# A scan, a routed expert layer and a Fourier mix in one kernel: the routing's PE steps, the last scatters and three small pieces of work in another order

## The chip, the cores and the metric

The kernel runs on one core of a Trainium2 chip. A core has five engines that work from queues of their own, each in the order in which the program was written: TensorE (PE, matrix products; PEld is its loading of weights), VectorE (DVE), ScalarE (ACT), GpSimd (POOL), and SyncE (SP), which here only issues DMAs. GpSimd issues the indirect DMAs (scatters by row number). An instruction waits at the head of its queue until its operands are there and its output's buffer is free, and whatever is behind it waits too. The metric is device time in microseconds (us), the median of several runs.

## The reference, cut to what matters

Three stages follow each other, each on the whole output of the one before (batch 4, 768 positions, width 256).

```
# 1. a scan with decay: 8 heads of 32, state 16; x, a, B, C are inputs, chunks of the sequence are carried by a state
y[i] = sum over j <= i in the chunk of (C_i . B_j) * exp(cum_i - cum_j) * x[j]  +  C_i . state * exp(cum_i)
state = decay_full * state + sum over j of B_j x_j * exp(cum_last - cum_j)
# 2. routing to one of 8 experts per token, with a gate that may keep the previous token's expert
fresh = argmax(x @ w_gate);  e = fresh if s == 0 or sigmoid(x @ w_local) < 0.5 else previous e
out = softmax(x @ w_gate)[e] * (relu(x @ w1[e]) @ w2[e])           # w1: 256 x 1024, w2: 1024 x 256
# 3. mixing and a feed-forward layer
u = x + real(fft(fft(x, axis=1), axis=2));  un = layernorm(u)
out = u + relu(un @ w_ch1) @ w_ch2                                 # 256 x 1024, 1024 x 256
```

## The kernel before, in words

The order of all work is written out by hand: the code is run once in the order in which it stands, and each engine's queue gets its instructions in that order.

**The scan** (0 to about 88 us) goes over 12 pairs: six chunks of 128 positions, and in each the batches 0, 1 and 2, 3. In pair i PE makes the scores of pair i+1 (L438, tiles `g`), the sums of pair i over the chunk (L469, into `yb`), which ScalarE copies to `x1t` (L476), the products for the state of pair i+1 (`state_mm`, L484, into the PSUM bank `mb`), and then two products of the rows of pair i (`tl`, L522, which read `x1t`) around the carry (L458). VectorE meanwhile makes the masks of the next pair (`mt`, L446), which the sums read.

**The routing** of a chunk that is done runs beside the following pairs. It is a generator cut into steps: "v" steps (VectorE's, called by `gap()`) and "p" steps (PE's, called by `place()`). A first "p" step transposes the keep-and-fresh numbers `kd` (L560), which ScalarE copies to `kr` (L570); VectorE scans them; a second transposes the result (L581), copied to `f_` (the chosen expert) by ScalarE at L583; VectorE makes a one-hot array of it (L593) and running counts; a third multiplies (L608, L609) to get ranks; VectorE turns ranks into row numbers `si` (L636). All "p" steps write to the same PSUM bank `mb` as the state products. Each turn of the pair loop calls `place()` three times, once near the beginning (ahead of the sums) and twice between the row products; a chunk's routing therefore goes forward by a "p" step at each. The last chunk is routed in two halves of two batches.

When `si` is there, GpSimd scatters a batch's 128 rows to `xs_buf`, a buffer in HBM ordered by expert (L643, by `leave()` or at the end). Behind the scatters of the last but one chunk, SP loads the first 256 rows of expert 0 from there into `xe` (L649); the scatters of the last chunk (four, one per batch) follow.

**The experts** run in turn: 0 on the 256 rows in `xe`, then 0 to 7 on the rest of their rows, which SP loads once the last scatter has landed. For each, the rows are transposed (L979) and split in a high and a low part (ScalarE, VectorE L982); weights come by SP and are split too, high by ScalarE (L207) and low by VectorE (L210). Products with the first weights (L918, tiles `mm`) turn in three PSUM buffers; ScalarE takes the relu `hh` (L924), VectorE the low part `hl` (L925); products with the second weights follow (L960). Expert 0's remaining 128 rows go another way: 12 products (L896), relu `hr` (L901), transposes (L908). A `hook(i)` is called behind each of 12 steps of an expert (or of a group of the mixing stage); tables say which piece of side work is issued in which hook (`PREP`, `SORT`, `plan`). Side work is among others the splitting of eight chunks of constants (`prep_steps`: VectorE L144 to L147, ScalarE L153, GpSimd L157 and L158), and the sort that prepares the two last experts (`sort_rows`, scatters to `xs_part` at L1054).

**The mixing stage**: `stage_b(b, k2)` (L1429) makes two products into a PSUM buffer `mix`, from which VectorE and ScalarE read; the last layer's results are `o` (VectorE, L1511). Products with the constants are again L918 and L960.

Of the kernel before, what the change touches and what calls it, by code (L numbers as in the profile page):

```python
# [16 lines left out]
NC = S // 128  # L17
# [7 lines left out]
EARLY = 256  # L25
# [7 lines left out]
MORE = {0: 8, 1: 10}  # L33
PREP = tuple((c, (e, 6), (e, 9)) for c, e in enumerate((1, 2, 3, 4, 5)))
PREP += ((5, (NE - 2, 7), (NE - 2, 9)), (6, (1, 9), (1, 10)), (7, (NE - 2, 9), None))
SORT = {(1, 8): 2, (1, 9): 1, (1, 10): 3, (2, 8): 2, (2, 9): 1, (2, 10): 3}

FT = (
    (((0, 0),), ((0, 1),)),
# [19 lines left out]
def tile_kernel(ctx: ExitStack, tc: tile.TileContext, io):  # L59
# [41 lines left out]
    def disjoint(name, w):  # L101
        if name in groups:
            tc.declare_no_dep(w.ins, group=name, reason="the rows of a scatter are its own")
        groups.add(name)
        tc.add_to_no_dep_group(name, w.ins)
# [13 lines left out]
    def prep_steps(i, pool):  # L119
        n = 512  # L120
        w = i // 4
        q = i % 4
        if w == 0:
            src = io["wc1"][(q // 2) * 128:(q // 2) * 128 + 128, (q % 2) * n:(q % 2 + 1) * n]
            dst = [t[:, q // 2, (q % 2) * n:(q % 2 + 1) * n] for t in wch[0:2]]
            sh = [128, n]
            raw = wraw.tile([128, n, 2], I32, tag="raw", name="rawc")
            SP.dma_start(out=raw.rearrange("p f t -> p (f t)"), in_=src.bitcast(I32))
        else:
            src = io["wc2"][q * 256:q * 256 + 256, :]  # L130
            dst = [t[:, 2 * q:2 * q + 2, :] for t in wch[2:4]]
            sh = [128, 2, D]
            raw = wraw.tile([128, n, 2], I32, tag="raw", name="rawc")
            SP.dma_start(
                out=raw.rearrange("p (k d) t -> p k (d t)", k=2),
                in_=src.bitcast(I32).rearrange("(k p) d -> p k d", p=128),
            )
            dst = [t.rearrange("p k d -> p (k d)") for t in dst]
        yield
        hw, lw = raw[:, :, 1], raw[:, :, 0]  # L140
        v = pool.tile([128, n], I32, tag="cv", name="cv")
        e = pool.tile([128, n], I32, tag="ce_", name="ce_")
        r = pool.tile([128, n], FP32, tag="cr", name="cr", bufs=1)
        V.tensor_scalar(out=e, in0=hw, scalar1=3, scalar2=0x3FFFFFF8, op0=ALU.logical_shift_left, op1=ALU.bitwise_and)  # L144
        V.scalar_tensor_tensor(out=v, in0=hw, scalar=-0x40000000, in1=e, op0=ALU.bitwise_and, op1=ALU.bitwise_or)
        V.tensor_scalar(out=e, in0=v, scalar1=-0x800000, scalar2=None, op0=ALU.bitwise_and)
        V.scalar_tensor_tensor(  # L147
            out=r, in0=lw.bitcast(mybir.dt.uint32), scalar=2.0 ** -52, in1=e.bitcast(FP32), op0=ALU.mult, op1=ALU.mult
        )
        vf = v.bitcast(FP32)  # L150
        if i == 6:
            yield
        A.activation(out=dst[0], in_=vf, func=ACTF.Copy)  # L153
        yield
        ef = e.bitcast(FP32)
        eng = G if i else V
        eng.tensor_tensor(out=ef, in0=vf, in1=dst[0], op=ALU.subtract)  # L157
        eng.tensor_tensor(out=dst[1], in0=ef, in1=r, op=ALU.add)  # L158
        yield

# [84 lines left out]
    def phase_a():  # L245
        with ExitStack() as st:
# [281 lines left out]
            def routing(c, b0, nb):  # L528
# [112 lines left out]
                def leave(bb):  # L641
                    for b in bb:
                        w = G.indirect_dma_start(  # L643
                            out=xs_buf, out_offset=bass.IndirectOffsetOnAxis(ap=si[:, b:b + 1], axis=0),
                            in_=x1n[:, b0 + b, 0:RW], in_offset=None, bounds_check=NE * NTOK - 1, oob_is_err=False,
                        )
                        disjoint("xs", w)
                    if c + 2 == NC and bb[-1] + 1 == nb:
                        SP.dma_start(out=xe, in_=xs_buf[0:EARLY, :].rearrange("(t p) r -> p t r", p=128))  # L649

                for b in range(0, nb, 2):
                    scq.append((leave, range(b, b + 2), now[0]))
# [63 lines left out]
            for i, (c, bp) in enumerate(pairs):  # L716
                now[0] += 1
                more = i + 1 < NP
                last = i + 2 >= NP
# [17 lines left out]
                if more:  # L737
                    scores(i + 1)
                if not last:
                    place()  # L740
                    prep(i + 2)
                intra(i)
                keep(i)
                if last:
                    place()
                if not more:
                    next(ws)
                if not more:
# [392 lines left out]
    def experts():  # L1141
# [4 lines left out]
            next(od)  # L1146
        xn = load_x(pools, 0)
        xn1 = load_x(pools, 1)
        keep_clock(ps2, 4)
        early = split_t((xp, pst), lambda t, d: xe[:, t, 137 * d:137 * d + 128], n=EARLY)  # L1150
        for _ in ws:
# [3 lines left out]
        def first(i):  # L1155
            nonlocal nxt, ws
            if 0 < i < 4:
                next(od)
            if i == 0:
                ws = load_w(1)  # L1160
            if i == 6:
                past(out_e, cc("rid")[:, 0:2], nfirst.to_broadcast([128, 2]))
                tokens(ids_e, xe, out_e, 2)
            if i == 8:
                nxt = split_x(pools, xn, out_of[:, 0, :], CAPS[0])
# [3 lines left out]
        for e in range(NE):  # L1169
# [7 lines left out]
            def hook(i):  # L1177
                nonlocal nxt, ws, nr
                if (e, i) in ((1, 0), (2, 4)):
                    srt[:] = [sort_rows(pools, SORTED[e - 1])]  # L1180
                    next(srt[0])
                for _ in range(SORT.get((e, i), 0)):
                    next(srt[0])
                if (e, i) == (1, 9):
                    sq = sm.tile([128, 1], FP32, tag="sq", name="sq", bufs=1)
                    A.activation(out=sq, in_=ident[:, 0:1], func=ACTF.Sqrt)
                if (e, i) == (4, 8):
                    nr = rounds(sm)
                    next(nr)
                if (e, i) == (4, 10):  # L1190
                    nr = next(nr)
                at = AT.get(e, (2, 3, 4, 5, 8, 8))
                for _ in range(at.count(i) if more else 0):
                    next(ws, None)
                for c, x, y in PREP:
                    if (e, i) == x:
                        chunk[c] = prep_steps(c, sm)
                        next(chunk[c])
                    if (e, i) == y:
                        next(chunk[c])  # L1200
                        if c != 6:
                            next(chunk[c])
                if (e, i) == (1, 11):
                    next(chunk[6])
                    next(chunk[6])
                if more and (e, i) == (e, MORE.get(e, 9)):
                    next(ws, None)
                    ws = load_w(e + 2) if e + 2 < NE else None
                if i == 7 and more:
                    nxt = split_x(pools, xn, out_of[:, e + 1, :], CAP if e + 1 == last - 1 else CAPS[e + 1])  # L1210
# [57 lines left out]
    def transform(lead):  # L1268
# [303 lines left out]
        def turn(i):  # L1572
# [39 lines left out]
        plan = {  # L1612
# [3 lines left out]
        }  # L1616
        for g, b in ((2, 2), (3, 3)):
            for k, v in (
# [136 lines left out]
```

## Time and profile before

| | |
|---|---|
| median of 3 runs | 424.89 us (423.1 to 426.29) |
| the profiled execution | 426.76 us, span 425.0 us, mean granted clock 0.996 |
| PE busy | 402.1 us, 95% of the span |
| PEld | 353.8 us, 83% |
| DVE | 281.8 us, 66% |
| ACT | 188.3 us, 44% |
| POOL | 147.7 us, 35% |
| chain that ended last | PE 74%, DVE 12%, ACT 6%, DMA 5%, issue 2% |

The span is the time from the first to the last record of the profiled execution; its device time is 1.8 us longer. Busy times are those in which an engine worked on an instruction; they overlap between engines. The chain is followed back from the last instruction to what released each step, so its shares tell what the end depended on, not what was busy. Rows of a timeline tell, in brackets, how long an engine had been idle before an instruction and what released it.

### The profile page before, as it was taken

To read this page: it belongs to the slowest core of one execution; us is meant where nothing else is said; L and a number is where in the kernel's file an instruction comes from. 1 tells how busy PE (TensorE), PEld (TensorE's weight loads), DVE (VectorE), ACT (ScalarE), POOL (GpSimd) and SP (SyncE) were. 2 spreads that over 40 slices of the span, in tenths; PEclk is the share of its full clock that TensorE was granted. 3 is DMA by queue.
4 is the path that set the end of the run, shared out by engine and by line. 5 is a ranking of instruction groups with operands and counts; after the bars stand their busy time and mean duration, and the time that the engine had idled before them with its cause. 6 is when DMAs were issued, how large, how long until landed. Compare 5 with 4: busy or idle time off the path is not lost.

```text
span 425.0 us, 8313 instructions
## 1 busy us (share of the span) xinstructions
PE 402.1 (95%) x3113; PEld 353.8 (83%) x3113; DVE 281.8 (66%) x770; ACT 188.3 (44%) x409; POOL 147.7 (35%) x206
## 2 busy tenths in 40 slices
PE   8898898788799999999999999999999999999995
PEld 4576566568689989999998998798898998989885
DVE  4678878873577897676865668875576685743431
ACT  3355465523656546474675425423324344331220
POOL 1264876641001717533253606325402713200000
PEclk9999999999899999999999999999999999999999
DMA  8798454224782957586663410452113010000101
GB/s 278 245 325 279 133 173 140 78 77 148 235 280 93 261 182 238 165 260 219 168 225 99 135 56 28 139 184 56 56 39 87 15 39 0 28 25 14 37 15 42
DMA packets 34089, 56.26 MB, mean 132 GB/s; under 512 B 3318, under 2 KB 23063, under 8 KB 34040
## 3 DMA queue, kind: packets, MB, share of 16 engines
q1 hardware_dynamic: 30328, 46.82, 34.7%
q0 software_dynamic: 3200, 8.54, 5.7%
q8 instruction: 26, 0.43, 0.4%
q10 hardware_dynamic: 512, 0.28, 0.2%
q14 instruction: 23, 0.19, 0.1%
HBM read 42.60 MB, written 13.17 MB: 131 GB/s over the span
## 4 chain that ended last, share of the span: by engine, by line
PE 74%; DVE 12%; ACT 6%; DMA 5%; issue 2%; POOL 0%; SPq 0%; ACTq 0%; DVEq 0%
PE mm L918 25%; PE mm L960 20%; PE mm L936 9%; PE tl L522 3%; DMA r<-in_w_dram 3%; PE tp L979 2%; PE f L1371 2%; DVE mt L446 2%; PE g L438 2%; PE mb L286 2%; PE yb L469 1%; DVE w1l L210 1%; DVE hl L925 1%; ACT w1h L207 1%; ACT x1t L476 1%
## 5 line engine op out<-in xcount | busy, mean ns | idle before, releaser
L925 DVE SCALAR_TENSOR_TENSOR hl<-mm,hh 128x512 fp32r<-128x512 f32 (+7 forms) x112 | 65.9, 593 | 48.2 <-ACT hh L924 47.9
L924 ACT ACTIVATE hh<-mm 128x512 fp32r<-128x512 f32 (+7 forms) x112 | 57.5, 521 | 72.6 <-PE mm L918 72.6
L960 PE MATMUL mm<-c2h,hh 128*128 128x256 f32 x192 | 54.4, 283 | 0.0
L960 PE MATMUL mm<-c2h,hl 128*128 128x256 f32 x192 | 53.8, 280 | 0.1
L960 PE MATMUL mm<-c2l,hh 128*128 128x256 f32 x192 | 53.6, 279 | 0.0
L918 PE MATMUL mm<-xh,w1h 128*128 128x288 f32 (+6 forms) x128 | 41.9, 335 | 1.8 <-DVE hl L925 1.4
L1075 POOL DMA_INDIRECT y_tok<-y,ids x26 | 26.9, 1034 | 45.3 <-ACT y L1074 23.3
L918 PE MATMUL mm<-xh,w1l 128*128 128x288 f32 (+6 forms) x128 | 40.5, 323 | 0.0
L918 PE MATMUL mm<-xh,c1h 128*128 128x512 f32 x96 | 38.8, 404 | 0.1
L918 PE MATMUL mm<-xh,c1l 128*128 128x512 f32 x96 | 38.0, 396 | 0.0
L960 PEld LDWEIGHTS mm<-c2h,hl 128*128 128x128 f32 x192 | 36.1, 188 | 0.3 <-DVE hl L925 0.3
L960 PEld LDWEIGHTS mm<-c2l,hh 128*128 128x128 f32 x192 | 36.1, 188 | 0.1
L960 PEld LDWEIGHTS mm<-c2h,hh 128*128 128x128 f32 x192 | 36.1, 188 | 0.1
L446 DVE TENSOR_TENSOR mt<-g,ca 128x512 f32<-128x512 f32 x48 | 31.4, 677 | 4.8 <-PE g L438 4.7
L918 PE MATMUL mm<-xl,w1h 128*128 128x288 f32 (+6 forms) x128 | 31.2, 324 | 0.0
L210 DVE TENSOR_TENSOR w1l<-r,w1h 128x512 fp32r<-128x512 f32 x32 | 24.3, 763 | 10.0 <-ACT w1h L207 9.8
L918 PE MATMUL mm<-xl,c1h 128*128 128x512 f32 x96 | 30.1, 395 | 0.0
L643 POOL DMA_INDIRECT xs_buf<-scr,si x24 | 24.5, 1021 | 13.3 <-DVE who L852 5.0
L918 PEld LDWEIGHTS mm<-xh,w1h 128*128 128x128 f32 x128 | 24.0, 188 | 4.6 <-DVE hl L925 2.9
L960 PE MATMUL mm<-w2h,hh 128*128 128x256 f32 (+1 forms) x96 | 27.4, 293 | 0.2 <-ACT hh L911 0.2
L1511 DVE SCALAR_TENSOR_TENSOR o<-mm,ve,home 128x256 f32<-128x256 f32 x24 | 11.6, 483 | 23.7 <-PE mm L960 23.6
L960 PE MATMUL mm<-w2l,hh 128*128 128x256 f32 (+1 forms) x96 | 26.6, 285 | 0.0
(337 smaller groups left out, 981.6 us busy)
## 6 DMA issues: line engine op xcount, KB each, us to landing
r<-in_w_dram SPq DMA_DIRECT2D x16, 1024.0 KB
rawc<-in_wc_dram SPq DMA_DIRECT2D x8, 512.0 KB
out_dram<-o SPq DMA_DIRECT2D x24, 128.0 KB
home<-y_tok SPq DMA_DIRECT2D x3, 768.0 KB
xs_buf<-scr SPq DMA_DIRECT2D x8, 265.0 KB
c1h<-in_x_dram SPq DMA_DIRECT2D x4, 512.0 KB
c2h<-in_bt_dram SPq DMA_DIRECT2D x6, 256.0 KB
c2l<-in_bn_dram SPq DMA_DIRECT2D x6, 256.0 KB
```

The source lines that it names most:

```text
L210: V.tensor_tensor(out=l_[:, x:y], in0=r_[:, x:y], in1=h[:, x:y], op=ALU.subtract)
L286: PE.matmul(out=ps[:, 0:w], lhsT=wrm[:, 0:128], rhs=wrm[:, 0:w], start=True, stop=True)
L446: V.tensor_tensor(out=m[:, :, 2 * q:2 * q + 2, :], in0=gp[q], in1=cc("cmask").unsqueeze(1).unsqueeze(1).to_broadcast([128, 2, 2, 128]), op ...
L522: PE.matmul(out=tl[:, 128 * g:128 * g + 137], lhsT=x1t[:, g, u, :], rhs=ca[:, o:o + 137], start=(g == 0), stop=(g == 1), skip_group_check= ...
L643: w = G.indirect_dma_start(out=xs_buf, out_offset=bass.IndirectOffsetOnAxis(ap=si[:, b:b + 1], axis=0), in_=x1n[:, b0 + b, 0:RW], in_offse ...
L918: PE.matmul(out=ps[:, 0:n], lhsT=w[:, d, f * 128:(f + 1) * 128], rhs=x[:, d, 0:n], start=(k == 0), stop=(k == 5))
L924: A.activation(out=hf, in_=ps[:, 0:n], func=ACTF.Relu)
L925: V.scalar_tensor_tensor(out=hl[:, f, 0:n], in0=ps[:, 0:n], scalar=0.0, in1=hf, op0=ALU.max, op1=ALU.subtract)
L936: PE.matmul(out=ps[:, 0:n], lhsT=w[:, f, 128 * d:128 * d + 128], rhs=h[:, f, 0:n], start=(k == 0), stop=(k == 23),)
L960: PE.matmul(out=ps[0:m, :], lhsT=h[:, f, t * 128:t * 128 + m], rhs=w[:, f, :], start=(k == 0), stop=(k == 23))
L1075: w = G.indirect_dma_start(out=y_tok, out_offset=bass.IndirectOffsetOnAxis(ap=ids[0:m, t:t + 1], axis=0), in_=y[0:m, :], in_offset=None, b ...
L1511: V.scalar_tensor_tensor(out=o, in0=ps, scalar=st_[b]["rs"][:, k:k + 1], in1=st_[b]["u"][:, k].rearrange("p t d -> p (t d)"), op0=ALU.mult ...
```

## The change

- `intra` and `keep` (the sums L469 and the copy `x1t`) are now issued ahead of the pair's first `place()` in every pair, as before only in the last two. Pairs 3 to 9 are those in which that `place()` finds a "p" step.
- The four last scatters and the load of `xe` are declared independent of each other.
- The call that loads expert 1's weights stands earlier in the code; SP's queue has the same DMAs in the same sequence.
- The low part of chunk 6 (two operations) goes from GpSimd to VectorE, one behind each of the first two steps of expert 2.
- The sort's steps of expert 2 come one hook later.
- One of the two mixings in hook 10 of group 0 of the last stage goes to hook 11.

```diff
--- before.py
+++ after.py
@@ -33,7 +33,7 @@
 MORE = {0: 8, 1: 10}
 PREP = tuple((c, (e, 6), (e, 9)) for c, e in enumerate((1, 2, 3, 4, 5)))
 PREP += ((5, (NE - 2, 7), (NE - 2, 9)), (6, (1, 9), (1, 10)), (7, (NE - 2, 9), None))
-SORT = {(1, 8): 2, (1, 9): 1, (1, 10): 3, (2, 8): 2, (2, 9): 1, (2, 10): 3}
+SORT = {(1, 8): 2, (1, 9): 1, (1, 10): 3, (2, 9): 2, (2, 10): 1, (2, 11): 3}
 
 FT = (
     (((0, 0),), ((0, 1),)),
@@ -153,8 +153,10 @@
         A.activation(out=dst[0], in_=vf, func=ACTF.Copy)
         yield
         ef = e.bitcast(FP32)
-        eng = G if i else V
+        eng = V if i in (0, 6) else G
         eng.tensor_tensor(out=ef, in0=vf, in1=dst[0], op=ALU.subtract)
+        if i == 6:
+            yield
         eng.tensor_tensor(out=dst[1], in0=ef, in1=r, op=ALU.add)
         yield
 
@@ -645,8 +647,11 @@
                             in_=x1n[:, b0 + b, 0:RW], in_offset=None, bounds_check=NE * NTOK - 1, oob_is_err=False,
                         )
                         disjoint("xs", w)
+                        if c + 1 == NC:
+                            tc.declare_no_dep(w.ins, group="xe", reason="ranks from the early count on; the load's rows past it are not used")
                     if c + 2 == NC and bb[-1] + 1 == nb:
-                        SP.dma_start(out=xe, in_=xs_buf[0:EARLY, :].rearrange("(t p) r -> p t r", p=128))
+                        w = SP.dma_start(out=xe, in_=xs_buf[0:EARLY, :].rearrange("(t p) r -> p t r", p=128))
+                        tc.add_to_no_dep_group("xe", w.ins)
 
                 for b in range(0, nb, 2):
                     scq.append((leave, range(b, b + 2), now[0]))
@@ -737,12 +742,10 @@
                 if more:
                     scores(i + 1)
                 if not last:
-                    place()
                     prep(i + 2)
                 intra(i)
                 keep(i)
-                if last:
-                    place()
+                place()
                 if not more:
                     next(ws)
                 if not more:
@@ -1146,6 +1149,7 @@
             next(od)
         xn = load_x(pools, 0)
         xn1 = load_x(pools, 1)
+        w1 = load_w(1)
         keep_clock(ps2, 4)
         early = split_t((xp, pst), lambda t, d: xe[:, t, 137 * d:137 * d + 128], n=EARLY)
         for _ in ws:
@@ -1157,7 +1161,7 @@
             if 0 < i < 4:
                 next(od)
             if i == 0:
-                ws = load_w(1)
+                ws = w1
             if i == 6:
                 past(out_e, cc("rid")[:, 0:2], nfirst.to_broadcast([128, 2]))
                 tokens(ids_e, xe, out_e, 2)
@@ -1200,8 +1204,7 @@
                         next(chunk[c])
                         if c != 6:
                             next(chunk[c])
-                if (e, i) == (1, 11):
-                    next(chunk[6])
+                if (e, i) in ((1, 11), (2, 0), (2, 1)):
                     next(chunk[6])
                 if more and (e, i) == (e, MORE.get(e, 9)):
                     next(ws, None)
@@ -1612,7 +1615,7 @@
         plan = {
             (0, 2): ((1, 0, 1), (1, 1, 1)), (0, 3): ((1, 0, 1),), (0, 4): ((1, 0, 1),), (0, 5): ((1, 1, 1),),
             (0, 6): ((1, 1, 1),), (0, 7): ((1, 2, 1),), (0, 8): ((1, 2, 4),), (0, 9): ((1, 2, 2),),
-            (0, 10): ((1, 2, 2),), (1, 8): ((1, 2, 5),), (1, 9): ((1, 2, 1),),
+            (0, 10): ((1, 2, 1),), (0, 11): ((1, 2, 1),), (1, 8): ((1, 2, 5),), (1, 9): ((1, 2, 1),),
         }
         for g, b in ((2, 2), (3, 3)):
             for k, v in (
```

PE in pair 6 of the scan, before (`kd` is the routing's array, `er` its scanned result):

```order
L438 MATMUL g_772<-ch,c2h 128x256
L438 MATMUL g_773<-ch,c2h 128x256
L560 MATMUL mb<-ca,kd 4x128 x2
L469 MATMUL yb<-mt,xt 32x128 x16
L484 MATMUL mb<-xt,c2l 64x128 x4
L522 MATMUL tl<-ca,x1t 128x137 x2
L458 MATMUL yb<-ce,st_155 128x128 x4
L581 MATMUL mb<-ca,er 128x4
L522 MATMUL tl<-ca,x1t 128x137 x2
```

and with the change:

```order
L440 MATMUL g_772<-ch,c2h 128x256
L440 MATMUL g_773<-ch,c2h 128x256
L471 MATMUL yb<-mt,xt 32x128 x16
L562 MATMUL mb<-ca,kd 4x128 x2
L486 MATMUL mb<-xt,c2l 64x128 x4
L524 MATMUL tl<-ca,x1t 128x137 x2
L460 MATMUL yb<-ce,st_155 128x128 x4
L583 MATMUL mb<-ca,er 128x4
L524 MATMUL tl<-ca,x1t 128x137 x2
```

The two transposes of `kd` have moved behind the sums into `yb`, and stand directly ahead of the state products into `mb`. In pairs 4 and 8 it is the same; in pair 3 the one transposed `er` moves in this way, and in pairs 5, 7 and 9 the rank products (L608 and L609 before).

POOL at the end of the scan, before, with the semaphores that each instruction waits for. `DMAHW6` is that of the load of `xe`:

```order
L585 COPY scr<-cb 128x2 [waits DVE_49,Activation_49]
L643 DMA xs_buf<-scr,si 24576x265 [waits DMASW4_49,DMAHW6_49,DVE_49,Pool_49]
L643 DMA xs_buf<-scr,si 24576x265 [waits DMASW5_49]
L643 DMA xs_buf<-scr,si 24576x265 [waits DMASW6_49,DVE_49,Pool_49]
L643 DMA xs_buf<-scr,si 24576x265 [waits DMASW7_49]
L1075 DMA y_tok<-y,ids_e 3072x256 [waits DMASW0_49,DVE_49,Activation_49]
```

and with the change:

```order
L587 COPY scr<-cb 128x2 [waits DVE_49,Activation_49]
L645 DMA xs_buf<-scr,si 24576x265 [waits DMASW4_49,DVE_49,Pool_49]
L645 DMA xs_buf<-scr,si 24576x265 [waits DMASW5_49]
L645 DMA xs_buf<-scr,si 24576x265 [waits DMASW6_49,DVE_49,Pool_49]
L645 DMA xs_buf<-scr,si 24576x265 [waits DMASW7_49]
L1078 DMA y_tok<-y,ids_e 3072x256 [waits DMASW0_49,DVE_49,Activation_49]
```

The first of the four scatters no longer waits for `DMAHW6`; what the others wait for is unchanged.

DVE in the first steps of expert 2, before (`cv`, `ce_`, `cr` belong to chunk 6, `mm` and `hl` to the expert, `w1l` to the weights of expert 3):

```order
L147 SCALAR_TENSOR_TENSOR cr<-rawc,ce__1998 128x512
L925 SCALAR_TENSOR_TENSOR hl<-mm_2048,hh 128x448
L925 SCALAR_TENSOR_TENSOR hl<-mm_2057,hh 128x448
L925 SCALAR_TENSOR_TENSOR hl<-mm_2066,hh 128x448
L925 SCALAR_TENSOR_TENSOR hl<-mm_2075,hh 128x448
L210 TENSOR_TENSOR w1l<-r_2004,w1h 128x512
L925 SCALAR_TENSOR_TENSOR hl<-mm_2088,hh 128x448
```

and with the change:

```order
L147 SCALAR_TENSOR_TENSOR cr<-rawc,ce__1998 128x512
L928 SCALAR_TENSOR_TENSOR hl<-mm_2046,hh 128x448
L157 TENSOR_TENSOR ce__1998<-cv,c2h 128x512
L928 SCALAR_TENSOR_TENSOR hl<-mm_2056,hh 128x448
L160 TENSOR_TENSOR c2l<-ce__1998,cr 128x512
L928 SCALAR_TENSOR_TENSOR hl<-mm_2066,hh 128x448
L928 SCALAR_TENSOR_TENSOR hl<-mm_2075,hh 128x448
L212 TENSOR_TENSOR w1l<-r_2004,w1h 128x512
L928 SCALAR_TENSOR_TENSOR hl<-mm_2088,hh 128x448
```

The two operations of the low part stand between the first three `hl`; on POOL they are gone.

## Rows read from the trace of the kernel before

**Rows 1.** Timeline, scan's end: start us, us, engine, line, instruction [idle before].
```profile
88.10 0.16 DVE L636 SCALAR_TENSOR_TENSOR si<-f__1287,rk 128x2 int32<-128x2 f32 x1
...
88.14 0.38 SPq L649 DMA_DIRECT2D xe<-xs_buf  x1
...
91.75 0.98 POOL L643 DMA_INDIRECT xs_buf<-scr,si  x1 [4.98 <-DVE who L852]
```
**Rows 2.** Chain that ended last, by time: start us, us, what.
```profile
95.61 4.09 DMA xs_buf<-scr,si
...
101.86 6.91 DMA r<-in_w_dram
...
117.21 10.56 PE mm L918 x48
...
228.32 2.81 PE mm L896 x12
...
236.39 6.39 PE mm L918 x48
```
**Rows 3.** Timeline, the first experts.
```profile
102.54 0.44 PE L979 MATMUL tp<-ca,xn 128*128 128x128 f32 x2 [1.10 <-DMA xn<-xs_buf]
...
108.88 1.06 ACT L207 ACTIVATE w1h<-r 128x1024 fp32r<-128x1024 f32 x1 [2.58 <-DMA r<-in_w_dram]
...
110.47 1.15 PE L908 MATMUL tp<-ca,hr 128*128 128x128 f32 x8 [1.89 <-ACT hr L901]
```
**Rows 4.** Windows: us, busy PE, PEld, DVE, ACT, POOL; clock, DMA share, GB/s.
```profile
93.00:94.00 1.00, 1.00 (x9) 0.90 (x9) 0.21 (x1) 0.32 (x1) 0.97 (x1) 1.00 0.38 136
...
113.00:114.00 1.00, 1.00 (x7) 1.00 (x6) 0.85 (x3) 0.97 (x3) 0.00 (x0) 0.50 0.00 0
```
**Rows 5.** Timeline, pair 3 of the scan.
```profile
31.46 0.17 ACT L583 ACTIVATE f__486<-mb 128x4 f32<-128x4 f32 x1 [0.25 <-PE g L438]
...
31.91 0.21 DVE L593 TENSOR_TENSOR ot<-cb,f__486 128x32 f32<-128x32 f32 x1
...
32.42 0.60 ACT L476 ACTIVATE x1t<-yb 128x512 f32<-128x512 f32 x1
...
33.07 0.73 PE L522 MATMUL tl<-ca,x1t 128*128 128x137 f32 x4 [0.19 <-ACT x1t L476]
```
**Rows 6.** Timeline, pair 4 (first row) and pair 6.
```profile
37.51 0.27 PE L560 MATMUL mb<-ca,kd 128*4 128x128 f32 x1 [0.67 <-DVE kd L555]
...
48.66 1.37 DVE L555 SCALAR_TENSOR_TENSOR kd<-kd,ff 128x4 f32<-128x4 f32 x1
...
50.09 0.27 PE L560 MATMUL mb<-ca,kd 128*4 128x128 f32 x1 [1.50 <-DVE kd L555]
...
50.39 0.37 ACT L570 ACTIVATE kr<-mb 4x256 f32<-4x256 f32 x1 [2.08 <-PE mb L560]
...
51.30 0.66 PE L484 MATMUL mb<-xt,c2l 128*64 128x128 f32 x8
...
52.21 0.73 PE L522 MATMUL tl<-ca,x1t 128*128 128x137 f32 x4 [0.26 <-ACT x1t L476]
```
**Rows 7.** Timeline, pair 9.
```profile
67.44 0.41 PE L608 MATMUL mb<-ot,cb 128*128 128x32 f32 x2
...
68.01 1.08 PE L469 MATMUL yb<-mt,xt 128*32 128x128 f32 x32
```
**Rows 8.** Page's costliest groups: low parts of weights (busy, mean ns | idle).
```profile
L210 DVE TENSOR_TENSOR w1l<-r,w1h 128x512 fp32r<-128x512 f32 x32 | 24.3, 763 | 10.0 <-ACT w1h L207 9.8
```
**Rows 9.** Timeline, start of expert 2.
```profile
146.93 2.22 DVE L210 TENSOR_TENSOR w1l<-r,w1h 128x512 fp32r<-128x512 f32 x1 [0.32 <-ACT w1h L207]
...
147.28 1.31 POOL L157 TENSOR_TENSOR ce__1998<-cv,c2h 128x512 f32<-128x512 f32 x1
...
149.74 0.47 PE L918 MATMUL mm<-xh,w1h 128*128 128x448 f32 x1 [0.69 <-DVE hl L925]
```
**Rows 10.** Timeline, the second mixing in hook 10.
```profile
291.27 0.49 PE L1429 MATMUL mix<-fb,home 128*128 128x129 f32 x2 [0.53 <-DVE xl L982]
```

## The prediction, as it was made

> **What bounds the kernel now.** I read the page first (TensorE, PE, is busy nearly throughout and holds most of the chain of waits), then PE's gaps by stage, then for each gap the chain and the timelines of the engines it waits for. PE's gaps lie in three places: the scan (0 to 88 us), the start of the experts (88 to 117 us), and a few single ones after that, which is all that a change of order can win.
>
> The start of the experts is the dearest. Expert 0's early half needs `xe`, loaded at 88.14, and the four scatters of the last chunk had their first row numbers at 88.26 (88.10 plus 0.16), but GpSimd started the first at 91.75, after 4.98 idle [rows 1]. The trace names another releaser; the order names the load of `xe`. The last scatter started at 95.61 and took 4.09 to land; all that SP issues next stands behind it: expert 0's rows, and at 101.86 the weights of expert 1, which landed 6.91 later, at 108.77 [rows 2]. So PE waited 1.10 for those rows; then ScalarE sat at the first weight copy (108.88, 2.58 idle), with the activation that PE wanted queued behind it, and PE stood still for 1.89 until 110.47 [rows 3]. Two and a half microseconds on the granted clock was 0.50, the lower level of 1.2 GHz [rows 4].
>
> In the scan a pair's PE work is a cycle: scores, attention sums (L469), the ScalarE copy `x1t`, the state products (L484), two row products (L522) around the carry. The routing's PE steps stand in that cycle, and PE is in order: in pair 6 `kd` was ready only at 50.03 (VectorE's L555 took 1.37), PE waited 1.50 for it, and the attention sums, which had everything, stood behind [rows 6].
>
> **The change, part by part.**
>
> *Last scatters.* Without the wait the first can start at about 88.4. The four keep their distance of (95.61 - 91.75) / 3 = 1.29, so the last starts at 92.25, 3.36 earlier [rows 1, 2]. The third needs row numbers of its own, which VectorE has long before its turn. SP's loads follow by as much. Expert 0's rows, which ended PE's wait at 102.5, come at about 99.1, and PE asks for them at 102.54 - 1.10 = 101.44: 1.10 saved. The weights land at 105.4, their copy of 1.06 ends at 106.5, and PE's products before the stop end at 110.47 - 1.89 - 1.10 = 107.5: ScalarE is free first. For the rest of that stage I take the same stage of expert 6, which has no late weights: from the end of its L896 products (228.32 + 2.81 = 231.13) to the next expert's first product at 236.39 it took 5.26; expert 0's took 117.21 - 108.58 = 8.63 [rows 2, 3]. Saved: 3.37, clock included. Together 4.5.
>
> Against that stands `xe`, whose load now shares the DMA engines with the scatters. One scatter keeps them busy for about 0.38 of a microsecond [rows 4]; one surely falls before `xe` lands, at most four do: 0.4 to 1.5 lost, or nothing if the load was not what PE waited for. I take 0.4, since the second scatter starts 1.29 later. Net **4.1**; ends 1.1 (only the wait for rows goes) and 4.5.
>
> The Trainium skill ("DMA: Bandwidth & Descriptors", section "Issuing engines are not separate DMA queues") says that DMAs issued from different engines run on the same 16 DMA engines and interleave. That speaks against this part, and the trace cannot contradict it, as it has no scatter beside the `xe` load; by it the loss is not nothing, and the case at its far end is the first rival.
>
> *The code move of expert 1's weight load* changes nothing in SP's order: the same loads in the same sequence. Nothing.
>
> *The scan.* Seven pairs (3 to 9) change, of three kinds.
> - Pair 3: the product L581 and its ScalarE copy `f_` move behind `x1t`. The state products share the PSUM bank and wait for that copy. `x1t` ended at 33.02; with `f_` (0.17) and the products (0.66, as in pair 6) the row products start at 33.85 instead of 33.07: **0.8 lost** [rows 5, 6]. Behind it VectorE loses more: its L593 waits for `f_`, started at 31.91, can now start at about 33.2, and the masks are queued behind it: 1.3 late.
> - Pairs 4, 6, 8: the attention sums no longer wait for `kd`; `kr` now stands behind `x1t`, and the state products wait for `kr` as before. In pair 6 the sums move up by more than a microsecond, `x1t` is done before `kd`, `kr` stays at 50.39 to 50.76, and the row products can start at 50.76 + 0.66 = 51.4 instead of 52.21: 0.8 saved [rows 6]. In 4 and 8 the stall was under half as long (0.67 in pair 4, same rows; pair 8 reads like it) and `kr` must wait for `x1t`, so I put them at half, 0.4 each: 1.6 in all.
> - Pairs 5, 7, 9: L608 and L609 go behind the sums, which start 68.01 - 67.44 = 0.57 earlier [rows 7]. In pair 9, which has no state products, all of it counts: 0.6; in 5 and 7 those products end where they did, and only the wait for `x1t` behind them goes, about half: 0.3 each. 1.2 in all.
>
> Sum: 2.8 saved, 0.8 lost, 2.0. From it comes VectorE's lateness from pair 3, which delays the next `kd`: nothing to 1.3; I take the middle, 0.7, as VectorE idles a little in each pair. Net **1.3**; ends 2.0 and a loss of 0.8 (pair 3's alone, the rest covered by VectorE).
>
> *Chunk 6's low part.* Its two GpSimd operations leave GpSimd. The first ran from 147.28 for 1.31, the VectorE subtraction begun at 146.93 took 2.22 where such a one takes 0.76 on average, and PE then waited 0.69 [rows 8, 9]. VectorE gets two operations of about 0.76 instead, one behind each of expert 2's first two `hl`; `hl` is needed three products later, since three PSUM buffers turn, so they hide unless VectorE is over a microsecond late. **0.7**; ends 0 and 0.7.
>
> Here row and rule part. The Trainium skill ("SBUF — State Buffer", section "Who interferes with whom") says that whichever of VectorE and GpSimd starts first holds the shared port for the whole instruction and the other blocks. The VectorE subtraction is recorded as starting first, and it was the slow one, GpSimd's was not; the measurement decides. By the rule the stall would have another cause and this term would be 0.
>
> *The sort of expert 2 and the later mixing.* The sort's steps go one hook later: two tiny products and VectorE's short operations; its scatters to `xs_part` are read two experts on. Nothing, unless GpSimd's queue behind them runs late, a few tenths. The second mixing of (0, 10) waited 0.53 for VectorE's split to free a PSUM buffer; behind the last tile's products that is long free [rows 10]: **0.5**; ends 0 and 0.5.
>
> **Sum.** 4.1 + 1.3 + 0.7 + 0.5 = 6.6. The profiled execution took 426.76 and would take 420.2; it stands 1.87 above the median of the runs, 424.89, so for the median I say **418.3**. With each term 10 to 20% off: 417.0 to 419.6.
>
> **Rivals.**
> - *The `xe` load pays.* All four scatters come in between: 1.5 lost instead of 0.4; 419.4. For it: they start within 0.3 of the load. Against: a scatter's data follow its start by a microsecond and more, and each comes 1.29 after the last. 0.10.
> - *The scan gains nothing.* VectorE is the bound there, pair 3's 0.8 is lost and nothing comes back: 2.1 less, 420.4. For it: VectorE is busier in the scan than anywhere. Against: PE's 1.50 is a wait for one step, not for a full engine. 0.15.
> - *The start's gain is given back.* The weights come 3.36 earlier and the next wait takes it: expert 1's stage needs its second weights and its split, made by ScalarE and VectorE in the same stretch. If only the wait for rows goes, 1.1 - 0.4 = 0.7 of the 4.1 is left: 421.7. Against: expert 6's stage, which has the same steps, took 5.26. 0.14.
> - *Slower.* The lateness that I see in pair 3 (1.3, an answer that reaches VectorE one `x1t` later) recurs at each of the seven moved places and never drains: 9.1 lost; the other terms give 5.3: 428.7. It decides from 0.8 per place on. For it: in four of the seven the state products now wait for a copy behind `x1t`. Against: in three of these `kd`, not `x1t`, comes last or nearly. 0.04.
>
> **Chances.** The forecast 0.57, the rivals as given. About 1% (4.2 us) is what a measurement of this kernel can tell from no change. Faster by more: the forecast, the first rival and a third of the second, 0.72. Slower by more: 0.05, the last rival and a little for what I have not seen. Within: 0.23. The range must take in the forecast with both ends of the small terms and most of the second and third rival: 415.8 to 422.0.
>
> **What would show it.** Right: no idle GpSimd between the last two sets of scatters, the last of them starting about 4 to 5 us earlier than 95.61 (3.36 and the scan's 1.3); no PE gap at the rows of expert 0 nor before L908, and the clock at its upper level throughout; `w1l` at some 0.7 in expert 2; no gap before the second mixing. In the scan: PE's waits at L560 gone, pair 3 longer by about 0.8, pair 9 shorter. Wrong: a gap before the transposes of `xe` (first rival), pairs 4 to 8 as long as before with VectorE full (second), a new gap between 105 and 125 us (third), a scan that ends after 88 us (last).

## The result, and the profile after

The changed kernel took **420.96 us** (median of 17 runs, 418.99 to 424.59), the kernel before 424.94 beside it: ratio 0.990 [0.987, 0.993], 4.0 us less. Here and below a ratio, its 95% interval in brackets and a mean clock leave out runs over 1.5% longer than the fastest of the same kernel. The forecast was 418.3, in a range of 415.8 to 422.0. The profiled execution is one of the longest, 424.37 us with a span of 422.6. The page's row of the granted clock, in tenths by 40 slices of the span, shows why:

```profile
PEclk9899989989999999999999999999999999999998
```

Three slices below 9 lie in the scan, where the kernel before had none (its one lies at the start of the experts). The windows tell how deep (us, busy time of PE, PEld, DVE, ACT, POOL; granted clock, DMA share, GB/s):

```profile
14.00:18.00 4.00, 3.66 (x18) 1.72 (x18) 0.88 (x2) 0.91 (x2) 0.23 (x1) 0.57 0.89 270
...
55.00:59.00 4.00, 4.00 (x30) 3.06 (x29) 1.84 (x7) 2.07 (x7) 3.51 (x5) 0.57 0.60 239
...
86.00:89.00 3.00, 3.00 (x7) 0.93 (x7) 2.63 (x11) 0.53 (x3) 2.39 (x3) 0.50 0.30 103
```

In each the clock fell to its lower level, 1.2 GHz, for 3.4 us, with PE busy nearly throughout. The 17 runs have mean clocks from 0.985 (the profiled one and another, 424.59) to 1.000 (three runs, 419.1 to 420.0).

**The start of the experts**: timeline rows of SP, VectorE, GpSimd and PE of the changed kernel.

```profile
90.77 0.38 SPq L653 DMA_DIRECT2D xe<-xs_buf  x1
...
91.68 0.16 DVE L638 SCALAR_TENSOR_TENSOR si<-f__1287,rk 128x2 int32<-128x2 f32 x1
...
92.62 0.98 POOL L645 DMA_INDIRECT xs_buf<-scr,si  x1 [2.75 <-issue]
...
96.48 0.98 POOL L645 DMA_INDIRECT xs_buf<-scr,si  x1 [0.30 <-issue]
...
95.08 0.60 PE L982 MATMUL tp<-ca,xe 128*128 128x128 f32 x4
...
104.87 0.38 PE L982 MATMUL tp<-ca,xn 128*128 128x128 f32 x2
...
110.69 0.60 PE L911 MATMUL tp<-ca,hr 128*128 128x128 f32 x4
...
116.06 0.38 PE L921 MATMUL mm<-xh,w1h 128*128 128x480 f32 x1
```

The first scatter starts 0.78 behind its row numbers (91.84) instead of 3.49 [rows 1]. The waits for expert 0's rows and ahead of L911 (L908 before) are gone [rows 3]. The transposes of `xe` follow PE's work without idle time, so PE did not pay for the load's company. The two ends of the stage in the kernel before:

```profile
91.49 0.60 PE L979 MATMUL tp<-ca,xe 128*128 128x128 f32 x4
...
117.05 0.38 PE L918 MATMUL mm<-xh,w1h 128*128 128x480 f32 x1
```

From the transposes of `xe` to expert 1's first product it took 117.05 - 91.49 = 25.56, and takes 116.06 - 95.08 = **20.98**.

**The scan**, from the scores issued in a pair to those issued in the next (first rows of L438, L440 after); in the changed kernel pairs 6 and 7 share a stretch of lower clock:

| pair | 3 | 4 | 5 | 6 | 7 | 8 | 9 |
|---|---|---|---|---|---|---|---|
| before | 5.35 | 6.27 | 5.48 | 7.10 | 5.47 | 6.55 | 5.48 |
| after | 6.21 | 5.99 | 5.22 | 7.59 | 5.80 | 6.56 | 4.91 |

PE in pair 3 and ScalarE and PE in pair 8 of the changed kernel:

```profile
34.47 0.22 PE L583 MATMUL mb<-ca,er 4*128 4x4 f32 x1
...
35.42 0.66 PE L486 MATMUL mb<-xt,c2l 128*64 128x128 f32 x8 [0.73 <-issue]
...
64.17 1.05 ACT L209 ACTIVATE w1h<-r 128x1024 fp32r<-128x1024 f32 x1
...
65.11 0.90 ACT L417 ACTIVATE ch<-ce,ca 128x256 f32<-128x256 f32 x2
...
65.91 0.58 ACT L478 ACTIVATE x1t<-yb 128x512 f32<-128x512 f32 x1
...
66.39 0.36 ACT L572 ACTIVATE kr<-mb 4x256 f32<-4x256 f32 x1
...
66.89 0.66 PE L486 MATMUL mb<-xt,c2l 128*64 128x128 f32 x8 [1.23 <-ACT ex L574]
```

In pair 3 the state products now wait 0.73, for the copy `f_` behind `x1t`. In pair 8 ScalarE makes the copy of a weight (L209), `ch`, `x1t` and `kr` back to back; PE's wait has only another name.

**The two late gaps**: VectorE in expert 2, and PE at the mixing that moved.

```profile
145.93 0.69 DVE L212 TENSOR_TENSOR w1l<-r,w1h 128x512 fp32r<-128x512 f32 x1 [0.30 <-ACT w1h L209]
...
291.62 0.38 PE L1432 MATMUL mix<-fb,home 128*128 128x129 f32 x2
```

The subtraction takes 0.69, where it took 2.22 with the GpSimd operation beside it [rows 9]; the mixing no longer waits [rows 10]. From expert 1's first product to expert 3's it takes 0.97 less, in the first group of the last stage 0.83 less.

### The profile page after: what moved, and what is told of

The parts are those of the page before. It is cut to its first block, busy times and chain, and to the rows that moved or that the text cites. A ratio compares the mean times of both kernels' runs of the same rounds, so it can differ in the third digit from the quotient of the medians.

```text
span 422.6 us, 8310 instructions
## 1 busy us (share of the span) xinstructions
PE 405.0 (96%) x3113; PEld 355.2 (84%) x3113; DVE 282.3 (67%) x772; ACT 188.1 (45%) x409; POOL 145.4 (34%) x204
## 4 chain that ended last, share of the span: by engine, by line
PE 81%; DVE 9%; ACT 4%; DMA 2%; issue 1%; POOL 0%; ACTq 0%; DVEq 0%
PE mm L921 27%; PE mm L963 21%; PE mm L939 9%; PE tl L524 3%; PE g L440 3%; PE tp L982 2%; PE f L1374 2%; PE mb L288 2%; PE yb L471 2%; DVE mt L448 2%; PE mm L899 1%; DMA r<-in_w_dram 1%; PE g L288 1%; PE yb L460 1%; DVE hl L928 1%
## 5 line engine op out<-in xcount | busy, mean ns | idle before, releaser
L212 DVE TENSOR_TENSOR w1l<-r,w1h 128x512 fp32r<-128x512 f32 x32 | 22.2, 700 | 7.7 <-ACT w1h L209 7.5
L939 PE MATMUL mm<-hh,w2h 128*128 128x288 f32 (+3 forms) x80 | 26.0, 325 | 0.0
```

Of the source, the lines that this page charges most:

```text
L212: V.tensor_tensor(out=l_[:, x:y], in0=r_[:, x:y], in1=h[:, x:y], op=ALU.subtract)
L939: PE.matmul(out=ps[:, 0:n], lhsT=w[:, f, 128 * d:128 * d + 128], rhs=h[:, f, 0:n], start=(k == 0), stop=(k == 23),)
```

## The experiments

They ran on three other chips, four kernels on each; on all three the kernel before took 433 to 434 us, with a mean clock of its runs of 0.979 to 0.986. Theories: **A**, the terms are real and the clock falls by chance, alike in both kernels; **B**, the new order makes it fall; **C**, the scatters' gain is given back; and, formed after the first four, **D**, the new order takes away a stop of PE behind which the clock falls.

**The kernel before, once more.** 

> The kernel before, unchanged, to see how time and granted clock scatter from run to run. Theory A (the four terms are real, and stretches of lower clock strike by chance, alike in both kernels): ratio 1.00 within 0.3%, mean clock of its runs about 0.995, as the changed kernel's 0.995. Theory B (the new order in the scan makes the clock fall more often): mean clock clearly higher than the changed kernel's, 0.997 or more.

 Ratio 0.9985 [0.995, 1.002]; mean clock of its 12 runs 0.980, of 23 more beside it 0.979. **The changed kernel.** 

> The changed kernel, unchanged, on the same chip as the others. Both theories: ratio about 0.990 (-4.0 us). Its new profile tells which stretches of lower clock recur: by A, others than 14 to 18, 55 to 59 and 86 to 89 us or none; by B the ones in the moved pairs (55 to 59) recur.

 Ratio **0.980 [0.976, 0.985]**, 424.33 us, mean clock 0.997. Here the change is worth twice as much, and the clock is higher with it: B fails, and A's "alike". The clock is not all of it: four runs of the kernel before with a mean clock of 0.991 to 0.994 took 431.5 to 432.0 us, the four of the changed kernel at 0.994 to 0.997 423.9 to 427.4. Pair 6 of the kernel before, on PE, ScalarE and VectorE ("remote": the profile knows no instruction as the releaser):

```profile
49.75 0.27 PE L560 MATMUL mb<-ca,kd 128*4 128x128 f32 x1 [0.68 <-DVE kd L555]
...
49.95 1.08 PE L469 MATMUL yb<-mt,xt 128*32 128x128 f32 x32
...
53.36 0.60 ACT L476 ACTIVATE x1t<-yb 128x512 f32<-128x512 f32 x1 [2.01 <-remote]
...
53.46 0.42 DVE L492 TENSOR_TENSOR sn<-mb,ca 128x256 f32<-128x256 f32 x1 [1.31 <-remote]
...
54.01 0.73 PE L522 MATMUL tl<-ca,x1t 128*128 128x137 f32 x4 [2.39 <-ACT x1t L476]
```

and of the changed kernel:

```profile
49.65 1.08 PE L471 MATMUL yb<-mt,xt 128*32 128x128 f32 x32
...
50.86 0.60 ACT L478 ACTIVATE x1t<-yb 128x512 f32<-128x512 f32 x1 [0.40 <-PE yb L471]
...
51.85 0.66 PE L486 MATMUL mb<-xt,c2l 128*64 128x128 f32 x8 [0.81 <-ACT ex L574]
...
52.44 0.73 PE L524 MATMUL tl<-ca,x1t 128*128 128x137 f32 x4
```

The sums begin at 49.95 and, by the model of their ends, take 1.08; but `x1t`, which waits for them, starts at 53.36, and PE stands still for 2.39. In the changed kernel `x1t` starts 1.21 behind the sums' start. In the kernel before, the clock stayed up behind that stop. It fell later in that scan, first 1.3 us behind a stop of PE in pair 9, then within one in pair 10 (two timeline rows, then windows, columns as above):

```profile
72.68 0.73 PE L522 MATMUL tl<-ca,x1t 128*128 128x137 f32 x4 [1.77 <-ACT x1t L476]
...
82.02 1.28 PE L522 MATMUL tl<-ca,x1t 128*128 128x137 f32 x4 [3.38 <-ACT x1t L476]
```

```profile
74.00:77.00 3.00, 3.00 (x22) 2.18 (x20) 0.95 (x6) 1.68 (x4) 0.19 (x1) 0.50 0.58 204
...
81.00:101.00 20.00, 18.55 (x86) 11.88 (x87) 12.45 (x59) 6.38 (x19) 6.18 (x8) 0.50 0.17 55
```

1.2 GHz for 3.4 us, and soon again for 20.5: the whole tail of the scan runs at the lower level, and PE reaches the transposes of `xe` at 104.25.

**Only the scatters.**

```diff
+                        if c + 1 == NC:
+                            tc.declare_no_dep(w.ins, group="xe", reason=...)
...
+                        w = SP.dma_start(out=xe, in_=...)
+                        tc.add_to_no_dep_group("xe", w.ins)
```

> The kernel before, and only the last scatters freed of the load of xe. Theory A: the stage from the transposes of xe to the first product of expert 1 falls from 25.6 to 21.0 us, time -4.0 to -4.6 us (420.5). Rival C (given back at the next wait, or the xe load pays): -0.7 to -1.5 us (423.5).

 Ratio 0.996 [0.993, 1.000], 1.6 us, mean clock 0.980. That is C's size, but not for C's reason: the stage takes 21.1 us, as A said, and it took 125.23 - 104.25 = 20.98 in the kernel before on this chip as well. With the clock down at the scan's end the row numbers themselves came late there, at 99.40, 3.65 behind the issue of the `xe` load (95.75), and the first scatter started 0.78 behind them, as in the changed kernel: there was no wait left to free. What the 1.6 us come from, the two profiles do not show. In this run the clock did fall right behind pair 6's stop, for 10.2 us:

```profile
54.53 1.28 PE L522 MATMUL tl<-ca,x1t 128*128 128x137 f32 x4 [2.37 <-ACT x1t L476]
```

```profile
55.00:64.00 9.00, 9.00 (x77) 6.82 (x76) 4.62 (x11) 2.93 (x8) 4.33 (x7) 0.50 0.44 139
```

**Only the scan.**

```diff
                 if not last:
-                    place()
                     prep(i + 2)
                 intra(i)
                 keep(i)
-                if last:
-                    place()
+                place()
```

> The kernel before, and only the routing's first products of a pair moved behind the sums. Theory A: pair 3 is 0.9 longer, pairs 4 to 7 and 9 shorter by 0.3 to 0.6 each, pair 8 the same; -1.2 us (423.7). Theory B: no gain in the median, 424.9 or above, with a mean clock at least 0.003 below that of the kernel before.

 Ratio **0.989 [0.984, 0.994]**, 4.7 us, mean clock 0.994: four times A's size, and the opposite of B. In its profile the old wait stands with the clock up on both sides:

```profile
96.31 0.60 PE L977 MATMUL tp<-ca,xe 128*128 128x128 f32 x4
...
106.94 0.44 PE L977 MATMUL tp<-ca,xn 128*128 128x128 f32 x2 [0.26 <-DMA xn<-xs_buf]
...
112.88 1.06 ACT L207 ACTIVATE w1h<-r 128x1024 fp32r<-128x1024 f32 x1 [2.18 <-DMA y_tok<-y,ids_e]
...
114.48 1.15 PE L906 MATMUL tp<-ca,hr 128*128 128x128 f32 x8 [1.49 <-ACT hr L899]
...
119.88 0.38 PE L916 MATMUL mm<-xh,w1h 128*128 128x480 f32 x1
```

119.88 - 96.31 = 23.57; in the changed kernel on this chip 114.99 - 94.05 = 20.94:

```profile
94.05 0.60 PE L982 MATMUL tp<-ca,xe 128*128 128x128 f32 x4
...
114.99 0.38 PE L921 MATMUL mm<-xh,w1h 128*128 128x480 f32 x1
```

So in this execution, where the first scatter started 3.25 behind its row numbers (96.32 - 93.07), the wait alone was worth **2.6**, not 4.5.

**The changed kernel again, and the three late edits alone** (the hunks of `prep_steps`, of its hook, `SORT` and `plan`). 

> The changed kernel once more, beside the two variants below and with another set of runs of the kernel before, whose granted clocks are listed too. Theory A (the terms are real, the clock falls by chance and alike): ratio 0.990 whatever the clock of the runs of before. Theory D (what the change is worth depends on how often the clock falls in the runs of before: the new order in the scan takes away the waits after which it falls): where the runs of before have a mean clock near 0.98 the ratio is about 0.980, near 0.995 it is about 0.990.

 Ratio 0.982 [0.979, 0.986], mean clock 0.995 against 0.981 beside it: D's number, and the second chip on which it comes out so. 

> The kernel before, and only the three late edits: chunk 6's low part on VectorE, the sort one hook later, the mixing behind the last tile. The prediction said -0.7, 0 and -0.5, so -1.2 us; the two profiles read -1.0 and -0.8, so -1.8 us (ratio 0.996). Expert 1's first product to expert 3's falls by 0.9, the first group of the last stage by 0.8. Rival (such gaps are made good at the next wait): 0.

 Ratio 0.991 [0.988, 0.995]. The two stages shrank as read, 44.90 to 43.96 and 30.62 to 29.71, together 1.85 us. The interval asks for 2.4 at least; the runs' mean clock was 0.003 higher than beside it, 1.2 us, and whether that is chance stays open.

**Pair 3 undone in the changed kernel**, on two chips.

```diff
+                if i == 3:
+                    place()
                 if not last:
                     prep(i + 2)
                 intra(i)
                 keep(i)
-                place()
+                if i != 3:
+                    place()
```

> The changed kernel with pair 3's product back ahead of the sums, as before. The step said that pair 3 loses 0.8 by its move: pair 3 takes 5.35 instead of 6.21 us again, time -0.9 us against the changed kernel. Rival (VectorE bounds the scan, so pair 4 takes it back): 0.

 

> The changed kernel with pair 3 alone undone, once more. If its first runs were no chance: ratio to the kernel before 0.977 to 0.981, some 0.9 us below the changed kernel's 0.980 to 0.982.

 Pair 3 takes 5.42 and 5.35 again, and pairs 4 to 9 take 37.0 and 37.3, as in the changed kernel's two profiles (37.3 and 36.8). The ratio is 0.979 [0.975, 0.982] on the chip on which the changed kernel has 0.982, and 0.983 [0.977, 0.990] on one on which it was not run: the gain is in the profile, but the runs scatter too much to show it.

**The routing half a pair later.**

```diff
-                yield "p", lambda: route["n"] >= c
+                yield "p", lambda: route["n"] >= c and route["late"]
...
-                yield "p", lambda: True
+                yield "p", lambda: route["late"]
                 rk_ps = ...
...
                 if not last:
+                    route["late"] = False
+                    place()
+                    route["late"] = True
                     prep(i + 2)
                 intra(i)
                 keep(i)
-                place()
+                if last:
+                    place()
```

> The changed kernel, with the routing half a pair later in pairs 4 to 9: the transposes of kd stand between the row products, the transpose of er ahead of the next pair's sums, the rank products between its row products, as pairs 2 and 3 had it before. If PE's waits ahead of the state products (0.7 to 1.3 in pairs 3, 4, 6, 8) are the price of the shared bank behind x1t, they go: -0.9 (pair 3) and -0.6 to -1.2 in each of pairs 4, 6, 8, together -3 to -4 us against the changed kernel. Rival (VectorE becomes the bound, or the later scatters delay the end of the scan): -1 to +1.

 Ratio 0.990 [0.986, 0.994], from 5 of its 12 runs, 0.8% above the changed kernel on the same chip: worse than even the rival said. Pairs 4 to 9 take 37.0, as before the edit: pairs 4 and 9 gain what 5 and 7 lose. PE's waits ahead of the state products were no price of their own; without them PE waits for `x1t` and VectorE's `sn`. And in the profiled execution, one of the seven longer ones, PE stood still for 4.9 us in pair 10, with the clock down for 17.1 from within that stop on. Whether that made the other runs long is not shown.

**Pair 6 alone**, moved in the kernel before, and undone in the changed one (as pair 3 above, with `i == 6`).

```diff
                 if not last:
-                    place()
+                    if i != 6:
+                        place()
                     prep(i + 2)
                 intra(i)
                 keep(i)
-                if last:
+                if last or i == 6:
                     place()
```

> The kernel before, with the moved product in pair 6 alone. On the chip of the experiments PE stands still for 2.4 us there, and the clock falls right behind it. Theory D (that stop lets the clock fall): pair 6 takes 6.0 instead of 8.4 us and the mean clock of the runs rises from 0.980 to 0.990 or more; -3.5 to -4.7 us, nearly all that the seven moves gave (ratio 0.989 to 0.992). Rival E (the clock falls after any of the gaps): -1 to -2.4 us with the clock at 0.98.

 Ratio **0.987 [0.981, 0.993]**, 5.5 us, mean clock 0.996 against 0.986 beside it: no less than all seven moves gave on the first of these chips. The stop itself is some 2.4 of it (the pair took 8.41 in the kernel before on that first chip, and takes 6.02 here); a clock higher by 0.010 is, by my estimate, at most 4.3 in an execution of 430. 

> The changed kernel with pair 6 alone undone. Theory D: the 2.4 us stop is back, the clock falls behind it at about 54 us, mean clock 0.985 or less; +3 to +5 us against the changed kernel (428 to 430, ratio 0.989 to 0.993). Rival E: +0.8 to 2.4 us, mean clock still 0.995 (ratio 0.983 to 0.987).

 Ratio **0.991 [0.987, 0.995]**, 1% above the changed kernel on the other chips; mean clock 0.992, between D's and E's. Pair 6 undone, on PE and ScalarE:

```profile
51.23 1.08 PE L471 MATMUL yb<-mt,xt 128*32 128x128 f32 x32
...
52.24 0.66 PE L486 MATMUL mb<-xt,c2l 128*64 128x128 f32 x8
...
54.72 0.60 ACT L478 ACTIVATE x1t<-yb 128x512 f32<-128x512 f32 x1 [2.08 <-remote]
...
55.37 1.28 PE L524 MATMUL tl<-ca,x1t 128*128 128x137 f32 x4 [2.46 <-ACT x1t L478]
```

and the windows from there on:

```profile
53.00:55.00 2.00, 0.00 (x0) 0.00 (x0) 0.62 (x2) 0.28 (x1) 1.84 (x3) 0.97 0.94 374
...
55.00:57.00 2.00, 1.63 (x8) 1.39 (x10) 0.84 (x2) 0.63 (x2) 1.53 (x3) 0.50 0.07 25
...
57.00:59.00 2.00, 2.00 (x13) 1.64 (x11) 0.77 (x2) 0.25 (x2) 1.99 (x3) 0.50 0.37 136
...
59.00:61.00 2.00, 2.00 (x17) 1.22 (x16) 1.43 (x3) 1.76 (x5) 1.43 (x4) 0.50 0.03 8
```

PE does nothing from 53 to 55, and the clock is at 0.50 behind it, for 6.8 us in all; the pair takes 10.13. With the move alone, in the kernel before:

```profile
51.43 0.66 PE L484 MATMUL mb<-xt,c2l 128*64 128x128 f32 x8 [0.81 <-ACT ex L572]
...
52.02 0.73 PE L522 MATMUL tl<-ca,x1t 128*128 128x137 f32 x4
```

```profile
53.00:55.00 2.00, 2.00 (x29) 1.59 (x25) 1.97 (x6) 1.08 (x5) 1.83 (x4) 1.00 0.64 246
...
55.00:57.00 2.00, 2.00 (x44) 1.48 (x36) 1.72 (x5) 1.05 (x3) 1.70 (x2) 1.00 0.22 74
```

6.02, at the full clock.

The move takes the stop away wherever it was profiled: on these chips `x1t` started 3.38 to 3.49 behind the sums' start in all four profiles with the transposes ahead of them, and 1.20 or 1.21 in all seven with the transposes behind. In three of the four the clock fell within the stop or right behind it, for 6.8 to 10.2 us; in the fourth, the kernel before, it did not. That, and the runs of the move alone, speak for D. The runs of the undoing speak less clearly: the changed kernel was not run on their chip, and against the nearest kernel there, that with pair 3 undone (0.983 [0.977, 0.990], mean clock 0.993), the undoing costs 3.2 us, or 2.4 if pair 3's 0.8 is taken off. D said 3 to 5, E 0.8 to 2.4.

**The scatters' wait kept in the changed kernel.** 

> The changed kernel with the wait of the last scatters on the load of xe kept. Theory D: with the clock up at the scan's end the wait shows, and the stage from the transposes of xe to expert 1 takes 23.6 instead of 21.0 us, +2.6 us (ratio 0.987 to 0.989); the 4.5 of the prediction held a stretch of lower clock of the profiled run. Rival (the wait is worth what the single edit gave on the kernel before): +1.3 us.

 Ratio 0.989 [0.984, 0.994], against 0.980 and 0.982 with the change whole on the other chips: 3 to 4 us; against pair 3 undone on the same chip, 2.3, or 1.5 with pair 3's 0.8 taken off. Between D and its rival that decides nothing. And the stage took 124.39 - 103.39 = 21.00 in the profiled execution, not D's 23.6: that was the longest run, 435.22 us, with the clock down from 79.9 to 100.8, so the row numbers came late again (98.56, the first scatter 0.77 behind them). The four profiles that show the wait's price are: first scatter 3.49 behind its row numbers, stage 25.56, with a fall of the clock in it (the kernel before, first chip); 3.25, 23.57 (only the scan); 2.41, 21.43 (pair 6 alone moved, 94.35 - 91.94 and 116.61 - 95.18); 0.78, 20.98 (the kernel before on the first of the other chips). The wait is worth what it is in the execution at hand, from nothing to over 2.6.

## Why the forecast held, and where it was mis-sized

By its steps, on the two profiles of the first chip:

- *Last scatters*: 4.58, where 4.5 was forecast; the `xe` load's price, put at 0.4, was nothing. The Trainium skill ("DMA: Bandwidth & Descriptors", section "Issuing engines are not separate DMA queues") has such transfers interleave on the same engines; whatever that cost the load, PE came 4.31 behind its issue (95.08 - 90.77), 3.35 before. The scatters themselves moved up by 2.71 against their row numbers (0.78 for 3.49), where 3.36 was put.
- *The scan*: pair 3 lost 0.86 (0.8); 4, 5 and 9 gained 0.28, 0.26 and 0.57 (0.4, 0.3, 0.6). Pairs 6 and 7 grew by 0.82 with 3.4 us at half speed in them, up to 1.7; some 0.9 gained (1.1). Pair 8 gained nothing where 0.4 was put: ScalarE's copy of a weight stands ahead of its `x1t`, which the forecast left out. Sum about 1.1, forecast 1.3.
- *Chunk 6* 0.97 (0.7), *the mixing* 0.83 (0.5); of the sort nothing is seen (expert 3's stretch 18.40 and 18.38). VectorE's operation was recorded as starting first and was the slow one, and without GpSimd's beside it, it takes 0.69: the row was right. The rule of the Trainium skill ("SBUF — State Buffer", section "Who interferes with whom") goes by which of the two issues first; the rows hold recorded starts, 0.35 apart, so no run here decides on it.

Together 7.5, of which 0.2 came back elsewhere: 426.76 - 7.3 = 419.5, and the three runs in which the clock never fell took 419.1 to 420.0. The terms are there. The step that failed is the last one of the sum, **that the difference of one execution carries over to the median**. The start's 3.37 was taken "clock included" from an execution in which the clock fell there [rows 4]; without a fall the wait was worth 2.6 in one execution of another chip, and here at least 2.9 (4.58 less at most 1.7 for the 3.4 us at half speed); and the median of before lay 1.87 below that execution. And no rival had the clock fall in the changed kernel, whose median lies 1.3 above the mean of its three runs without one. 6.6 + 0.7 - 1.9 - 1.3 = 4.1; measured 4.0. That the first chip's runs of before lost less to the clock than the profiled one is inferred from their times; their clocks were not recorded. Three signs that the prediction named did not show in the profiled execution: the clock was not at its upper level throughout; the last scatter started at 96.48, 0.87 later than before instead of 4 to 5 earlier, as the scan ended 3.6 later (91.68 against 88.10), with three falls of the clock in it; and PE still waits 0.76 for `kd` in pair 6, now behind the sums.

What the forecast did not see is what pair 6 can be worth: it was put at 0.8, and moved alone, on one of the three other chips, it gave 5.5, the stop and the clock together. On the first chip that stop was not there (PE waited 0.26 for `x1t` [rows 6]), and none of the edits was run alone.

## What to carry to other kernels

Split a term that holds a stretch of lower clock into its wait and its clock, and forecast the median from the wait alone. Don't put a product that waits for a late value ahead of products that have everything: the stop is paid twice when the clock falls behind it, as it did in three of four profiles here. And edits that pay in the same stretch don't add: the stage behind the scan had nothing to gain from the freed scatters in the executions whose scan ended at half speed.

## What was not expected of the hardware

On three chips PE's results came later than the model of its ends says, at the same place in each: the copy of pair 6's sums started 3.41, 3.38 and 3.49 behind their start (53.36 - 49.95; 53.72 - 50.34 with the late edits alone; 54.72 - 51.23) where the transposes of `kd` stood ahead of them, and 1.20 or 1.21 where they stood behind. It is not that the sums alone took long: VectorE's `sn`, which waits for the state products that PE issued behind the sums, started 0.10 behind that copy in all three (53.46, 53.82, 54.82), though those products take 0.66 of their own; the two results came to be seen at nearly one moment. Nor does it need the transposes ahead: in pair 10, where the sums stand first in every kernel, `x1t` came after 4.14 of ScalarE's idle time in the kernel before (81.38), after 5.99 with the routing half a pair later (81.02) and after 4.28 with the scatters' wait kept (80.54), and in all three the clock fell before it came. On the first chip the row products of pair 6 had waited only 0.26 for that copy [rows 6]. Why PE's results are late at these places, and on these chips, is open.
